# Moving the weight sums of a recursive matrix product from GpSimd to VectorE, and multiplying one pair of column tiles without them

## The chip, the cores and the metric

The kernel runs on one core of one Trainium2 chip. The metric is the device time of one execution in microseconds (us). Three runs of the kernel before took 566.07, 566.41 and 570.07 us; their median is 566.41 us. The profile is one further execution, of 565.62 us.

Five engines work side by side, each through its own queue in a fixed order: TensorE (PE; its weight loads are the row PEld), VectorE (DVE), ScalarE (ACT), GpSimd (POOL) and SyncE (SP, which issues DMA transfers). An instruction that has to wait holds up all behind it on its engine.

## The reference

Three parts follow one another. The first is a landmark attention over 4 batches of 576 tokens and 8 heads. Its 2304 rows of 512 go through a mixture of 8 experts in which a token is computed by one expert alone. The rows that come out go through a gated unit with 1536 hidden columns:

```python
gate = 1.0 / (1.0 + np.exp(-(x @ w_gate)))
val = x @ w_val
return (gate * val @ w_out).astype(np.float32)
```

Here `w_gate` and `w_val` are 512x1536 and `w_out` is 1536x512.

## The kernel before, in words

**Blocks.** A block is the 576 tokens of one batch together with one expert that some of them chose. Only blocks that are needed are computed. In this input there are three: "lead", "1" and "2". For each the kernel runs the expert (`expert_products`) and then the gated unit (`unit_products` or `fast_products`, then `unit_out`). A loop at the end, for further blocks ("b"), is in the program but has no iteration here. I call the gated units of the three blocks unit 0, unit 1 (the middle one) and unit 2.

**Precision.** Each fp32 operand is split into a high part (a cast by ScalarE) and a low part (a subtraction by VectorE). A product is three matmuls: high by high, high by low, low by high (`PASSES`). Weights lie split in six tiles `ws`, in the profile ws_69 to ws_72, ws_2646 and ws_2647. A unit's gate and value weights go through the first four and `w_out` through the last two (`fast_outs`).

**Tiles.** The unit's 1536 columns are 12 column tiles of 128 (`KG` = 12), numbered f, and the tokens two halves of 288. For each f and each half the unit makes a gate product and a value product over the inner dimension of 512, then sigmoid, a multiplication and another split into a `slot` tile (`gated_rows`). `unit_out` multiplies these with `w_out` into five accumulators `acc` in PSUM; the five are stored by indirect DMA from GpSimd (`store_out`, line 1089).

**The recursive product.** Unit 0 works plainly. Units 1, 2 and b (`FAST`) take two column tiles together, the pair p, as a 2x2 block product with 7 multiplications in place of 8 (`chain`, line 915). For each pair and for gate and value apart there are 7 pieces of weight, listed in `CHAIN`: three are blocks of the weights, one is a block that was overwritten by the sum S2 = A21 + A22 - A11 (`fast_combine`, line 767), and three more, s1, s3 and s4, are each the sum or difference of a block and S2. `fast_piece` (line 779) makes them in `temp` tiles, in the profile `rows`, before it splits them. All these sums are done by GpSimd, 128x256 elements each: 24 for the S2 of all pairs, once, and 36 for each fast unit. The moving operand too is summed, four sums "t1" to "t4" made by VectorE (`turn`). Split pieces go through 8 places in the four `ws` tiles, in turn: piece n waits until piece n - 8 has been multiplied (the event `used_...`).

A chain needs three PSUM banks of the three there are (`mm`); for the value chain of the first pair it uses three accumulators instead (`spare`). Results of the seven products are added up by VectorE and ScalarE (`fast_one`, `fast_five`, `fast_two`, `fast_gate`).

**What sets the order.** Every piece of work is a Python generator that names the engine and the events that it needs. `Streams.go` takes, step by step, the one that can start first by a table of costs and due times, and emits its instructions. The order on each engine is thus fixed when the program is built; on the chip each engine runs its list and waits where an operand is late. In the profile nearly all instructions have line 103, the helper that emits them, so the tile names tell them apart.

## Time and profile before

| what | value |
|---|---|
| median of three runs | 566.41 us |
| the profiled execution | 565.62 us |
| its span, first to last instruction | 563.7 us |
| mean granted TensorE clock | 0.981 of full speed |
| unit 1, first product of its block to the expert of block 2 | 272.1 to 407.9 us |
| expert of block 2 | 407.9 to 447.5 us |
| unit 2, up to the last matmul | 447.5 to 555.9 us |

Times in the views are us from the first instruction. A busy time of an engine is the time in which one of its instructions ran; a wait is idle time just before an instruction, put down to whatever released it last. An instruction of VectorE or ScalarE may be shown starting a little before the one ahead of it ends, so that a row of n merged instructions is shorter than n times one of them.

### The profile page before, as it was taken

How to read it: one execution, taken by the hardware profiler on the slowest of the kernel's cores; microseconds unless marked ns; L12 is line 12 of the kernel's file. 1: busy time of each engine (PE TensorE's matmuls, PEld its weight loads, DVE VectorE, ACT ScalarE, POOL GpSimd, SP SyncE). 2: the span in 40 equal slices, each digit the busy share in tenths (PEclk: the TensorE clock that was granted, in tenths of full speed). 3: DMA queues.
4: the chain of work that ended last, by engine and by line, in shares of the span. 5: the costliest groups of instructions: out<-in, count | busy, mean ns of one | idle time of the engine just before them, and what ended most of it. 6: DMA issues, size and time to landing. Idle time of an engine off the chain costs nothing.

```text
span 563.7 us, 12531 instructions
## 1 busy us (share of the span) xinstructions
PE 530.5 (94%) x4734; PEld 470.6 (83%) x4734; DVE 438.3 (78%) x1056; ACT 305.9 (54%) x777; POOL 162.8 (29%) x196
## 2 busy tenths in 40 slices
PE   7999979999999999999794999999999989999994
PEld 3468868889999899999684889998789989999983
DVE  7887767878599999898879898755375798888541
ACT  1645524454677777673454666743263467677331
POOL 2425844334311200000618643100240133331003
PEclk9999989999999999999887999999999999999998
DMA  8548885966345455530420000000530000000002
GB/s 314 193 138 307 295 297 152 316 198 211 121 150 187 153 192 180 187 117 2 169 77 19 1 1 2 1 1 0 185 126 2 1 1 2 1 1 1 1 1 90
DMA packets 33188, 61.90 MB, mean 110 GB/s; under 512 B 3584, under 2 KB 13440, under 8 KB 33120
## 3 DMA queue, kind: packets, MB, share of 16 engines
q1 hardware_dynamic: 32016, 57.48, 30.9%
q0 software_dynamic: 1104, 3.54, 1.8%
q8 instruction: 39, 0.64, 0.5%
q14 instruction: 29, 0.24, 0.1%
HBM read 47.76 MB, written 13.25 MB: 108 GB/s over the span
## 4 chain that ended last, share of the span: by engine, by line
PE 64%; DVE 15%; issue 11%; DMA 4%; ACT 3%; POOL 2%; SPq 1%; POOLq 0%; ACTq 0%; DVEq 0%
PE mm L103 42%; PE acc L103 14%; DVE ws L103 5%; DVE slot L103 2%; PE pz L103 1%; DMA w_raw<-in_moe_w 1%; DVE work L103 1%; PE pv L103 1%; DMA slot<-in_k 1%; ACT ws L103 1%; PE idle L103 1%; DMA x_rows<-xa 1%; DVE cvt_v L103 1%; DVE cvt_g L103 1%; PE pc L103 1%
## 5 line engine op out<-in xcount | busy, mean ns | idle before, releaser
L103 PE MATMUL mm<-xa,ws 128*128 128x288 f32 x966 | 139.9, 297 | 1.1 <-DVE slot L103 0.6
L103 PEld LDWEIGHTS mm<-xa,ws 128*128 128x128 f32 x966 | 132.6, 188 | 6.3 <-DVE slot L103 1.4
L103 PE MATMUL acc<-ws,slot 128*128 128x512 f32 x504 | 128.7, 396 | 2.4 <-DVE ws L103 1.7
L103 PE MATMUL mm<-slot,ws 128*128 128x288 f32 x840 | 124.0, 301 | 5.7 <-DVE ws L103 4.0
L103 PEld LDWEIGHTS mm<-slot,ws 128*128 128x128 f32 x840 | 116.4, 191 | 9.8 <-DVE ws L103 4.7
L103 PEld LDWEIGHTS acc<-ws,slot 128*128 128x128 f32 x504 | 91.2, 189 | 20.0 <-DVE ws L103 2.0
L103 PE MATMUL mm<-xb,ws 128*128 128x288 f32 x558 | 87.5, 301 | 1.9 <-ACT work L103 0.9
L103 PEld LDWEIGHTS mm<-xb,ws 128*128 128x128 f32 x558 | 79.7, 191 | 5.5 <-ACT work L103 1.3
L103 DVE TENSOR_TENSOR slot<-work,slot 128x288 fp32r<-128x288 f32 (+1 forms) x80 | 34.3, 453 | 14.5 <-ACT slot L103 14.1
L103 ACT CAST slot<-work 128x288 fp32r<-128x288 f32 x56 | 22.6, 431 | 38.4 <-PE acc L103 23.3
L103 DVE TENSOR_TENSOR ws<-wg_res,ws 128x256 fp32r<-128x256 f32 (+1 forms) x60 | 31.3, 536 | 10.7 <-ACT ws L103 10.2
L103 DVE TENSOR_TENSOR work<-mm,work 128x288 f32<-128x288 f32 x64 | 28.9, 452 | 11.2 <-PE mm L103 9.1
L103 ACT COPY work<-mm 128x288 f32<-128x288 f32 x66 | 26.1, 396 | 20.0 <-DVE mm L103 11.7
L103 DVE TENSOR_TENSOR ws<-rows,ws 128x256 fp32r<-128x256 f32 x72 | 34.5, 496 | 1.9 <-ACT ws L103 1.9
L103 POOL TENSOR_TENSOR rows<-wg_res,wg_res 128x256 f32<-128x256 f32 x24 | 19.8, 839 | 47.8 <-DVE ws L103 47.8
L103 DVE TENSOR_TENSOR ws<-wv_res,ws 128x256 fp32r<-128x256 f32 (+1 forms) x60 | 32.7, 557 | 1.0 <-ACT ws L103 0.9
L1089 POOL DMA_INDIRECT out<-rows,idx_lead x5 | 5.3, 1063 | 93.5 <-DVE rows L103 86.1
L103 ACT CAST ws<-wg_res 128x256 fp32r<-128x256 f32 (+1 forms) x60 | 25.4, 447 | 11.6 <-PE mm L103 8.6
L103 ACT CAST ws<-wv_res 128x256 fp32r<-128x256 f32 (+1 forms) x60 | 26.0, 447 | 10.0 <-PE mm L103 4.3
L103 POOL TENSOR_TENSOR ws<-w_raw,ws 128x512 fp32r<-128x512 f32 x16 | 20.9, 1307 | 26.9 <-ACT ws L103 21.1
L103 ACT CAST ws<-rows 128x256 fp32r<-128x256 f32 x72 | 27.6, 404 | 1.3 <-POOL rows L103 1.1
L103 ACT ACTIVATE slot<-mm 128x288 fp32r<-128x288 f32 x48 | 19.5, 409 | 16.2 <-PE mm L103 15.6
(248 smaller groups left out, 802.8 us busy)
## 6 DMA issues: line engine op xcount, KB each, us to landing
w_raw<-in_moe_w SPq DMA_DIRECT2D x48, 256.0 KB, 3.5
raw_g<-in_moe_w_gate SPq DMA_DIRECT2D x12, 512.0 KB, 3.6
raw_v<-in_moe_w_val SPq DMA_DIRECT2D x12, 512.0 KB, 3.5
raw_o<-in_moe_w_out SPq DMA_DIRECT2D x12, 512.0 KB, 4.0
out<-zeros SPq DMA_DIRECT2D x18, 256.0 KB, 5.1
vs<-in_v SPq DMA_DIRECT2D x8, 512.0 KB, 5.1
slot<-in_q SPq DMA_DIRECT2D x8, 288.0 KB, 5.5
slot<-in_k SPq DMA_DIRECT2D x8, 288.0 KB, 6.0
```

The lines of the kernel that those rows point to most:

```text
L103: return getattr(self.engine, op)(*args, **kwargs)
L1089: scatter = nc.gpsimd.indirect_dma_start(out[:, :], bass.IndirectOffsetOnAxis(ap=idx[0:n, c : c + 1], axis=0), o[0:n], None, bounds_check= ...
```

## The change

All sums move from GpSimd to VectorE: the 24 for S2 and the 36 of each fast unit. The first pair of column tiles of unit 1 (block "1", f below 2) is no longer a recursive product: a new function `pair` makes it of eight plain products, each over one column tile, one half of the tokens, gate or value. Its weights are the blocks themselves (eight pieces instead of 14), so it needs neither S2 nor the sums of the moving operand. S2 of pair 0, which overwrites the block A21, is made after unit 1 has split that block. Since unit 1 now uses 78 pieces and not 84, the places of the pieces and the tiles that the next expert takes first shift (`spread`, `ROLL_TWO`, `fast_out`), and the spare accumulators are no longer used in unit 1. Units 2 and b keep their seven products in all pairs.

```diff
@@ -678,7 +678,7 @@
     ROLL_LEAD = [i % 4 for i in range(KF // 2 + 2 * KD)]
 
     ROLL = [0, 1, 4, 5, 2, 3] * 2
-    ROLL_TWO = [2, 3, 4, 5, 0, 1] * 2
+    ROLL_TWO = [3, 0, 4, 5, 1, 2] * 2
 
     def unit_tiles(b, f):
 
@@ -722,21 +722,24 @@
     def unit_gate(b, f, half, pts):
 
         sl = slice(half * HT, (half + 1) * HT)
-        yield "act", "sg"
-        sg = tmp.tile([128, HT], F32, tag="sg", name="sg")
+        kind = "work" if b in FAST else "sg"
+        yield "act", kind
+        sg = work() if b in FAST else tmp.tile([128, HT], F32, tag="sg", name="sg")
         on.act.activation(sg, pts[0][:, 0:HT], AF.Sigmoid)
         run.release("bank")
         yield ("dve",)
         on.dve.tensor_tensor(sg, pts[1][:, 0:HT], sg, ALU.mult)
         run.release("bank")
         yield from gated_rows(b, f, half, sg)
-        run.release("sg")
+        if b in FAST:
+            works.append(sg)
+        run.release(kind)
         run.done(f"low_{b}{f}{half}")
 
     def gated_rows(b, f, half, sg):
         sl = slice(half * HT, (half + 1) * HT)
         k = f % 4
-        head = half == (f % 2 if b in FAST else 0)
+        head = half == (0 if plain(b, f) else f % 2)
         yield "act", *([f"slot{k}"] if head else [f"gv_{b}{f}"])
         if head:
             gvs[b, f] = slot(k).rearrange("p a t -> p (a t)")
@@ -757,7 +760,7 @@
 
     def spread(b):
 
-        return 4 if b in ("1", "2") else 0
+        return {"1": 4, "2": 6, "b": 0}[b]
 
     def fast_tile(b, n):
         j = (n + spread(b)) % 8
@@ -766,27 +769,30 @@
 
     def fast_combine():
 
-        for p in range(KG // 2):
+        for p in (*range(1, KG // 2), 0):
             for nm, res in zip("gv", (wgs, wvs)):
                 s2, a22, a11 = res[2 * p + 1][:, 0:2], res[2 * p + 1][:, 2:4], res[2 * p][:, 0:2]
-                begun = [f"used_1{14 * (p - 2)}"] if p > 1 else []
-                yield "pool", f"narrow_o{KG - 1}", f"u_0{nm}{2 * p}", f"u_0{nm}{2 * p + 1}", *begun
-                on.pool.tensor_tensor(s2, s2, a22, ALU.add)
-                yield ("pool",)
-                on.pool.tensor_tensor(s2, s2, a11, ALU.subtract)
+                begun = [f"u_1{nm}02"] if p == 0 else [f"narrow_o{KG - 1}"] if p == 1 else [f"used_1{14 * (p - 2)}"]
+                yield "dve", f"u_0{nm}{2 * p}", f"u_0{nm}{2 * p + 1}", *begun
+                on.dve.tensor_tensor(s2, s2, a22, ALU.add)
+                yield ("dve",)
+                on.dve.tensor_tensor(s2, s2, a11, ALU.subtract)
                 run.done(f"s2_{nm}{p}")
+
+    def plain(b, f):
+        return b not in FAST or (b == "1" and f < 2)
 
     def fast_piece(b, p, nm, i, n):
 
         res = {"g": wgs, "v": wvs}[nm]
         a11, a12, s2, a22 = (res[2 * p + j // 2][:, j % 2 * 2 : j % 2 * 2 + 2] for j in range(4))
         w = fast_tile(b, n)[1]
-        what = CHAIN[i]
+        what = ("11", "12", "s2", "22")[i] if plain(b, 2 * p) else CHAIN[i]
         if what in ("s1", "s3", "s4"):
             x, y, op = {"s1": (s2, a11, ALU.add), "s3": (a22, s2, ALU.subtract), "s4": (a12, s2, ALU.subtract)}[what]
-            yield "pool", "temp"
+            yield "dve", "temp"
             src = temps.pop(0)
-            on.pool.tensor_tensor(src, x, y, op)
+            on.dve.tensor_tensor(src, x, y, op)
         else:
             src = {"11": a11, "12": a12, "s2": s2, "22": a22}[what]
         yield ("act",)
@@ -804,15 +810,17 @@
         run.spawn(fast_outs(b), run.urgency)
         n = 0
         for p in range(KG // 2):
-            for nm in "gv":
-                for i in range(len(CHAIN)):
+            ways = [(nm, i) for nm in "gv" for i in range(len(CHAIN))]
+            if plain(b, 2 * p):
+                ways = [(nm, i) for j in range(2) for nm in "gv" for i in range(2 * j, 2 * j + 2)]
+            for nm, i in ways:
                     k, _ = fast_tile(b, n)
-                    yield None, f"s2_{nm}{p}", *([f"ws{k}"] if n < 8 and n % 2 == 0 else [f"used_{b}{n - 8}"] if n >= 8 else [])
+                    yield None, *([] if plain(b, 2 * p) else [f"s2_{nm}{p}"]), *([f"ws{k}"] if n < 8 and n % 2 == 0 else [f"used_{b}{n - 8}"] if n >= 8 else [])
                     run.spawn(fast_piece(b, p, nm, i, n), run.urgency)
                     n += 1
 
     def fast_out(b, f):
-        return 4 + f % 2 if f < KG - 2 else (4 - spread(b)) // 2 + f % 2
+        return 4 + f % 2 if f < KG - 2 else {"1": 1, "2": 1, "b": 2}[b] + f % 2
 
     def fast_outs(b):
         for f in range(KG):
@@ -912,16 +920,42 @@
 
         left = [KG]
 
+        count = (KG - 2 if plain(b, 0) else KG) * 7 + (8 if plain(b, 0) else 0)
+
+        def pair():
+            n = 0
+            for f in range(2):
+                tiles = {(nm, j): n + 2 * i + j for i, nm in enumerate("gv") for j in range(2)}
+                for half in range(2):
+                    pts = []
+                    for nm in "gv":
+                        for j in range(2):
+                            yield "pe+", *(["bank"] if j == 0 else []), f"u_{b}{nm}0{2 * f + j}", f"expert_{expert}", *[f"y_{expert}{2 * j + k}{half}" for k in range(2)]
+                            if j == 0:
+                                pts.append(bank())
+                            _, w = fast_tile(b, tiles[nm, j])
+                            for kk in range(2):
+                                for a, c in PASSES:
+                                    on.pe.matmul(
+                                        pts[-1][:, 0:HT], w[:, a, kk], x[:, c, 2 * j + kk, half * HT : (half + 1) * HT],
+                                        start=(j == 0 and kk == 0 and (a, c) == PASSES[0]), stop=(j == 1 and kk == 1 and (a, c) == PASSES[-1]),
+                                    )
+                            if half == 1:
+                                run.done(f"used_{b}{tiles[nm, j]}")
+                    run.spawn(unit_gate(b, f, half, list(pts)), run.urgency)
+                n += 4
+            run.done(f"banks_{b}v0")
+
         def chain(p, nm, order):
             q = f"{b}{nm}{p}"
             spare = p == 0 and nm == "v"
-            before = [f"expert_{expert}", *([f"f_{b}{d}1" for d in (1, 3)] if spare else [])] if p == 0 else [f"banks_{b}{'v' if nm == 'g' and p > 1 else 'g'}{p - (nm == 'g')}"]
+            before = [f"expert_{expert}", *([f"f_{b}{d}1" for d in (1, 3)] if spare else [])] if p == 0 else [f"banks_{b}{'v' if nm == 'g' and (p > 1 or plain(b, 0)) else 'g'}{p - (nm == 'g')}"]
             pts = {}
             for i, (pt, what, needs) in enumerate((
                 ("x", "11", before), ("z", "t1", []), ("x", "21", [f"one_{q}"]), ("z", "22", [f"five_{q}"]),
                 ("y", "t2", []), ("y", "t3", [f"two_{q}"]), ("y", "t4", [f"c22_{q}"]),
             )):
-                new, n = pt not in pts, order * len(CHAIN) + i
+                new, n = pt not in pts, order * 7 + i - (6 if plain(b, 0) else 0)
                 yield "pe+", *(([f"acc{len(pts)}"] if spare else ["bank"]) if new else []), f"u_{q}{i}", *ready(what), *needs
                 if new:
                     pts[pt] = (accs[len(pts)] if spare else bank())[:, 0:HT]
@@ -933,7 +967,7 @@
                             start=(new and kk == 0 and (a, c) == PASSES[0]), stop=(kk == 1 and (a, c) == PASSES[-1]), skip_group_check=True,
                         )
                 run.done(f"used_{b}{n}")
-                if n >= 7 * KG - 8 and n % 2:
+                if n >= count - 8 and n % 2:
                     run.release(f"ws{k}")
                 x, y, z = (f"acc{j}" if spare else "bank" for j in (0, 2, 1))
                 if i == 0:
@@ -955,7 +989,10 @@
                 run.done(f"unit_{b}")
 
         yield (None,)
-        for p in range(KG // 2):
+        if plain(b, 0):
+            left[0] -= 2
+            run.spawn(pair(), run.urgency)
+        for p in range(1 if plain(b, 0) else 0, KG // 2):
             for i, nm in enumerate("gv"):
                 run.spawn(chain(p, nm, 2 * p + i), run.urgency)
```

**TensorE at the start of unit 1.** `mm<-xb` are products of the block's own tokens, `mm<-slot_40..` those of the sums t1 to t4, `acc<-ws_26..` the output products of unit 0. Before:

```order
L103 MATMUL mm<-xa,ws_72 128x288 x12
L103 MATMUL mm<-xb,ws_71 128x288 x6
L103 MATMUL acc_2691<-ws_2646,slot_3982 128x512 x2
L103 MATMUL acc_2689<-ws_2646,slot_3982 128x512 x3
L103 MATMUL mm<-slot_4018,ws_71 128x288 x6
L103 MATMUL mm<-xb,ws_72 128x288 x6
L103 MATMUL acc_2691<-ws_2647,slot_4070 128x512 x2
L103 MATMUL acc_2689<-ws_2647,slot_4070 128x512 x3
L103 MATMUL acc_2687<-xb,ws_70 128x288 x6
L103 MATMUL mm<-xb,ws_72 128x288 x6
L103 MATMUL mm<-slot_4019,ws_69 128x288 x6
```

Now:

```order
L103 MATMUL mm<-xa,ws_72 128x288 x12
L103 MATMUL mm<-xb,ws_71 128x288 x12
L103 MATMUL mm<-xb,ws_72 128x288 x12
L103 MATMUL mm<-xb,ws_71 128x288 x12
L103 MATMUL mm<-xb,ws_72 128x288 x12
L103 MATMUL mm<-xb,ws_69 128x288 x12
L103 MATMUL mm<-xb,ws_70 128x288 x12
L103 MATMUL mm<-xb,ws_69 128x288 x12
L103 MATMUL mm<-xb,ws_70 128x288 x12
L103 MATMUL acc_2691<-ws_2646,slot_3982 128x512 x2
L103 MATMUL mm<-xb,ws_71 128x288 x6
L103 MATMUL mm<-slot_4018,ws_71 128x288 x6
```

The eight rows of 12 matmuls are the plain pair. They stand ahead of the first product of a sum, which before came as the second product of the unit.

**VectorE at the same place.** `rows<-` are the sums s1, s3 and s4, `wg_res<-` and `wv_res<-` those of S2, `ws<-` the low parts of the split pieces. Before:

```order
L103 TENSOR_TENSOR ws_69<-wv_res_2652,ws_69 128x256
L103 TENSOR_TENSOR ws_70<-wg_res_2654,ws_70 128x256
L103 TENSOR_TENSOR ws_71<-wg_res_2654,ws_71 128x256
L103 TENSOR_TENSOR ws_72<-wg_res_2657,ws_72 128x256
L103 TENSOR_TENSOR ws_69<-wg_res_2657,ws_69 128x256
L103 TENSOR_TENSOR ws_70<-rows_4015,ws_70 128x256
L103 TENSOR_TENSOR ws_2647<-wo_res_2653,ws_2647 128x512
L103 TENSOR_TENSOR work_4253<-acc_2689,work_4253 128x288
```

Now:

```order
L103 TENSOR_TENSOR wg_res_2663<-wg_res_2663 128x256
L103 TENSOR_TENSOR ws_71<-wg_res_2654,ws_71 128x256
L103 TENSOR_TENSOR rows_4015<-wg_res_2657,wg_res_2654 128x256
L103 TENSOR_TENSOR slot_4276<-work_4012,slot_4276 128x288
L103 TENSOR_TENSOR wg_res_2663<-wg_res_2663,wg_res_2660 128x256
L103 TENSOR_TENSOR ws_71<-rows_4015,ws_71 128x256
L103 TENSOR_TENSOR ws_72<-wg_res_2654,ws_72 128x256
L103 TENSOR_TENSOR rows_4015<-wg_res_2654,wg_res_2657 128x256
L103 TENSOR_TENSOR work_4014<-mm,work_4014 128x288
L103 TENSOR_TENSOR wv_res_2664<-wv_res_2664 128x256
L103 TENSOR_TENSOR ws_72<-rows_4015,ws_72 128x256
L103 TENSOR_TENSOR slot_4276<-work_4014,slot_4276 128x224
```

The sums now stand in VectorE's queue between the splits, the multiplications of gate and value and the splits of these.

**GpSimd at the same place.** Before, from the end of unit 0 on:

```order
L1089 DMA out<-rows_4015,idx_lead 2304x512
L1089 DMA out<-rows_4016,idx_lead 2304x512
L103 TENSOR_TENSOR rows_4015<-wg_res_2651,wg_res_2648 128x256
L103 TENSOR_TENSOR rows_4015<-wg_res_2648,wg_res_2651 128x256
L103 TENSOR_TENSOR rows_4016<-wg_res_2651 128x256
L103 TENSOR_TENSOR rows_4016<-wv_res_2652,wv_res_2649 128x256
L103 TENSOR_TENSOR wg_res_2663<-wg_res_2663 128x256
L103 TENSOR_TENSOR wg_res_2663<-wg_res_2663,wg_res_2660 128x256
```

Now:

```order
L1126 DMA out<-rows_4015,idx_lead 2304x512
L1126 DMA out<-rows_4016,idx_lead 2304x512
L1126 DMA out<-rows_4017,idx_lead 2304x512
L1126 DMA out<-rows_4015,idx_lead 2304x512
L1126 DMA out<-rows_4016,idx_lead 2304x512
L1126 DMA out<-rows_4017,idx_one 2304x512
L1126 DMA out<-rows_4015,idx_one 2304x512
```

Line 1126 is line 1089 of before. Between the stores of unit 0 and those of unit 1 GpSimd has nothing left to do.

## Rows read from the trace of the kernel before

**Rows 1.** The page's first part: busy time, share of the span and instructions of each engine.

```profile
PE 530.5 (94%) x4734; PEld 470.6 (83%) x4734; DVE 438.3 (78%) x1056; ACT 305.9 (54%) x777; POOL 162.8 (29%) x196
```

**Rows 2.** Busy time by stage: from:to, us, each engine's busy us (count), PEclk, DMA.

```profile
272.10:338.00 65.90, 52.74 (x321) 47.82 (x320) 60.14 (x110) 37.62 (x105) 39.58 (x48) 0.90 0.17 57
338.00:372.70 34.70, 34.70 (x245) 33.59 (x245) 27.13 (x70) 23.49 (x66) 7.46 (x9) 1.00 0.01 2
...
407.90:447.50 39.60, 38.90 (x289) 38.19 (x288) 26.62 (x53) 18.39 (x43) 8.84 (x10) 1.00 0.16 53
447.50:460.30 12.80, 10.99 (x77) 10.21 (x76) 11.62 (x26) 8.90 (x27) 2.98 (x4) 1.00 0.00 0
460.30:523.40 63.10, 63.10 (x439) 60.75 (x439) 53.14 (x138) 45.34 (x128) 20.31 (x24) 1.00 0.01 1
```

**Rows 3.** Timeline of TensorE: start, us, instructions merged, [idle before <-releaser].

```profile
243.15 20.05 PE L103 MATMUL mm<-xa,ws 128*128 128x288 f32 x150
...
280.94 1.33 PE L103 MATMUL mm<-slot,ws 128*128 128x288 f32 x4 [4.04 <-DVE ws L103]
...
297.75 0.73 PE L103 MATMUL acc<-ws,slot 128*128 128x512 f32 x2 [1.69 <-DVE ws L103]
...
303.16 1.33 PE L103 MATMUL acc<-slot,ws 128*128 128x288 f32 x4 [4.41 <-DVE ws L103]
...
382.97 12.89 PE L103 MATMUL acc<-ws,slot 128*128 128x512 f32 x56
395.80 1.95 PE L103 MATMUL mm<-w_raw,fold_now 64*32 64x128 f32 x64
```

**Rows 4.** Busy time in stretches of 5 us, as in Rows 2, around both stops.

```profile
275.00:280.00 5.00, 1.90 (x11) 1.45 (x9) 5.00 (x4) 1.32 (x4) 4.92 (x8) 0.90 0.93 313
280.00:285.00 5.00, 4.05 (x14) 3.77 (x15) 3.87 (x11) 3.71 (x11) 1.40 (x2) 0.50 0.69 245
...
300.00:305.00 5.00, 1.84 (x7) 1.84 (x8) 5.00 (x6) 0.80 (x2) 4.92 (x7) 0.50 0.00 0
305.00:310.00 5.00, 4.03 (x24) 3.45 (x24) 5.00 (x10) 2.12 (x7) 3.60 (x5) 0.87 0.00 0
```

**Rows 5.** Timeline of VectorE, columns as in Rows 3.

```profile
266.52 0.82 DVE L103 TENSOR_TENSOR work<-xb 128x288 f32<-128x288 f32 x2
...
273.98 4.25 DVE L103 TENSOR_TENSOR work<-work,work 128x288 f32<-128x288 f32 x1
...
282.45 0.41 DVE L103 TENSOR_TENSOR ws<-wg_res,ws 128x256 fp32r<-128x256 f32 x1
...
283.13 0.74 DVE L103 TENSOR_TENSOR ws<-rows,ws 128x256 fp32r<-128x256 f32 x2
...
297.85 4.38 DVE L103 TENSOR_TENSOR slot<-work,slot 128x224 fp32r<-128x224 f32 x2 [0.15 <-ACT slot L103]
...
544.53 1.90 DVE L103 TENSOR_TENSOR ws<-wo_res,ws 128x512 fp32r<-128x512 f32 x3
```

**Rows 6.** Timeline of GpSimd, columns as in Rows 3.

```profile
274.42 1.45 POOL L103 TENSOR_TENSOR rows<-wg_res,wg_res 128x256 f32<-128x256 f32 x2
```

**Rows 7.** VectorE's forms from 275 to 345 us: xcount, busy us, mean ns, idle before.

```profile
L103 DVE TENSOR_TENSOR ws<-rows,ws 128x256 fp32r<-128x256 f32 x24 | 12.5, 527 | 0.3 <-ACT ws L103 0.3
L103 DVE TENSOR_TENSOR ws<-wv_res,ws 128x256 fp32r<-128x256 f32 x15 | 9.7, 662 | 0.0
L103 DVE TENSOR_TENSOR ws<-wg_res,ws 128x256 fp32r<-128x256 f32 x15 | 9.0, 621 | 1.2 <-ACT ws L103 1.0
...
L103 DVE TENSOR_TENSOR slot<-work,slot 128x224 fp32r<-128x224 f32 x6 | 6.2, 1041 | 0.8 <-ACT slot L103 0.8
```

**Rows 8.** The same from 460 to 560 us.

```profile
L103 DVE TENSOR_TENSOR ws<-rows,ws 128x256 fp32r<-128x256 f32 x30 | 13.1, 461 | 0.8 <-ACT ws L103 0.8
...
L103 DVE TENSOR_TENSOR slot<-work,slot 128x224 fp32r<-128x224 f32 x12 | 4.6, 385 | 4.0 <-ACT slot L103 3.8
```

**Rows 9.** Timeline of VectorE, the last product of the block before unit 2.

```profile
447.71 0.71 DVE L103 TENSOR_TENSOR work<-mm,gate_now 128x288 f32<-128x288 f32 x1 [0.63 <-PE mm L103]
```

## The prediction, made before the changed kernel was run

> **What bounds the kernel now.** I read first the busy time of the engines. TensorE is busy for 530.5 of 563.7 us [rows 1], so a change can win little more than TensorE's idle time and what its clock loses, unless it takes matmuls away, and this one adds some.
>
> Then I read the stages, to see where TensorE idles. From 272.1 to 338.0 us, the first half of unit 1, it is busy for 52.74 of 65.90 us, so 13.2 us are idle, and the granted clock is 0.90 there. In the second half of unit 1 and in the middle of unit 2 it does not idle at all, although GpSimd makes the same sums there; the expert of block 2 loses 0.7 us and the start of unit 2 1.8 us [rows 2].
>
> Then the timeline of TensorE, to see what ended the idle time. Three stops, of 4.04, 1.69 and 4.41 us, make 10.1 of the 13.2 us, and each ended with a VectorE split of weights [rows 3]. Behind both long ones stands a stretch of 5 us at a granted clock of 0.50, that is at 1.2 in place of 2.4 GHz: half of the 4.05 and of the 1.84 us busy there was lost, 2.9 us, and the stretches at 0.90 and 0.87 give 0.2 and 0.5 us more [rows 4]. With 3.6 us of clock the first half of unit 1 loses 16.8 us in all.
>
> Last I read VectorE and GpSimd at the stops. One VectorE subtraction that reads two SBUF tiles started at 273.98 us and took 4.25 us, and two at 297.85 took 4.38; undisturbed, two of 288 columns take 0.82 us, so one about 0.45 [rows 5]. The long one started just before a run of GpSimd sums [rows 6]: in the five us from 275 to 280 GpSimd ran 8 instructions without a break and VectorE got through 4 [rows 4]. From 275 to 345 us the three forms of `ws` splits take 527, 662 and 621 ns on average and the 224-wide split 1041 ns [rows 7]; alone they take 410 ns [rows 5] and 385 ns [rows 8]. With the one of 4.25 us the excess is 24 x 0.117 + 15 x 0.252 + 15 x 0.211 + 6 x 0.656 + 3.8 = 17.5 us. So GpSimd's sums hold VectorE up, VectorE's splits come late, and TensorE stops.
>
> **The change, part by part.** *The sums on VectorE.* A 128x256 subtraction takes 0.41 us, and two in a row 0.74 [rows 5], so one more costs 0.34 us of the queue; in the same way 288 columns cost 0.82 - 0.45 = 0.37 us and 512 columns 0.61, from three in 1.90 [rows 5]; for a split of 224 and 64 together I take 0.43, in proportion. In unit 1 VectorE gets 23 sums for S2 and 30 for s1, s3, s4: 53 x 0.34 = 18.0 us. The excess of 17.5 us goes, since GpSimd runs only stores there, so in unit 1 the move is even for VectorE. What it wins is that no sum waits behind seven others, at 39.58/48 = 0.82 us each [rows 2], for splits that TensorE waits for.
>
> The Trainium skill ("SBUF — State Buffer", section "SBUF: two separate sides") says that VectorE with two SBUF inputs and GpSimd share one pair of ports, and that the loser is blocked for the whole of the other's instruction. By that the subtraction of 4.25 us would have been held for one sum, 0.74 us, and taken 1.2; the trace shows it held through several, and I go by the trace. By the rule alone the two long stops would be 3 us shorter each, as much less would be won, and the sum would be 561.6 us.
>
> *The plain pair.* Eight products of 12 matmuls in place of 14 of six: 96 - 84 = 12 matmuls more, each 20.05/150 = 0.133 us [rows 3]: 1.6 us on TensorE's path. On VectorE it saves six splits (14 pieces to 8) and six additions in PSUM, 6 x 0.34 + 6 x 0.37 = 4.3 us. It puts 12.8 us of products that need only single blocks ahead of the first sum.
>
> *Does VectorE keep up in unit 1?* I count the changed order from the last sum of `xb` halves. It stood at 266.52 + 0.37 = 266.9 us [rows 5]; now one S2 sum more and one 512-wide split less are ahead of it, so about 266.6. Up to the last piece stand 131 instructions of 256, 72 of 288, 10 of 512 and 8 pairs of 224 and 64: 80.7 us. Behind it TensorE has 6 matmuls of 0.133 us, 89 of 12.89/56 = 0.23 and twice the 64 small ones of the next expert, 1.95 us each [rows 3]: 25.2 us. So VectorE alone would end unit 1 at 266.6 + 80.7 + 25.2 = 372.5 us if it never waited, at 392.7 if it waited a fifth of the time. TensorE without any loss ends at 407.9 - 16.8 + 1.6 = 392.7 us. TensorE stays the bound as long as VectorE is packed to 80%; in the stalled stretch it was busy for 60.14 of 65.90 us, 91% [rows 2].
>
> The narrowest place is the first `w_out` split of unit 1. VectorE reaches its end after 45.7 us, at 312.3 without a wait and at 317.4 at 90%; TensorE starts on the pair at 272.1 + 18 x 0.133 = 274.5, behind the last products of unit 0, and wants the split after 43.0 us of products, at 317.5. At 85% TensorE would stop for 2.9 us there. The pair frees its eight places only at 274.5 + 6.4 = 280.9 and at 287.3 us, which holds VectorE up by some 2 us more. I take 2.0 us for that, 0.5 for the pair's own start (its value pieces come just as the gate product ends) and 1.5 for waits inside chains, half of what is left of the 13.2 us beside the three stops: **4.0 us stay** in unit 1. The bounds are 0, if everything fits, and 6.7, if VectorE is packed to 75%: 266.6 + 107.6 + 25.2 = 399.4.
>
> *Unit 2.* It gets 36 sums, 12.2 us, and gets little back: its splits take 461 ns [rows 8], some 50 over 410, in 69 instructions of three forms 3.5 us. At its start VectorE counts from the last gated product, at 447.71 us [rows 9], 9.1 us to the piece that TensorE wants 8.0 us after its own start at 447.5; that product ends 0.9 us after this start, so TensorE waits 2.0 us by this, 3.0 at 90%, where it waits 1.8 now. After that VectorE has 68.4 us in the queue up to the last piece and TensorE 84.8, so 81%; now it is busy for 53.14 of 63.10 us, 84%, and TensorE never idles [rows 2]. I take **1.5 us more** in unit 2; bounds 0, and 4.4 at 75%: 448.4 + 91.2 + 20.7 us of output products = 560.3 in place of 555.9.
>
> *The rest.* The 0.7 us in block 2's expert follow a VectorE write while GpSimd makes six sums; I take half, 0.4 us, as won. The eight S2 sums in unit 0 were hidden by TensorE's work there, which never stopped for long: 0. The stores come at the same points of the accumulators, and the tail is the same: 0.
>
> **The sum:** 565.6 - 16.8 + 1.6 + 4.0 + 1.5 - 0.4 = **555.5 us**. This is made against the profiled execution, 565.62 us, which lies 0.8 us under the median of 566.41; I leave that out.
>
> **The rivals.** *Everything is won.* Nothing stays in units 1 and 2: 565.6 - 16.8 + 1.6 - 0.7 = 549.7 us. For it speaks that TensorE idles nowhere in the second half of unit 1 [rows 2]; against it the narrow place above. Chance 0.15.
>
> *A mere swap.* VectorE pays for the sums what it is freed of, and TensorE goes on following it. Then unit 1 gets shorter only by what VectorE saves: 17.5 - 18.0 + 4.3 = 3.8 us, and unit 2 pays 1.5: 563.3 us, no change that can be told. Against it stands that TensorE's stops were bursts, two runs of sums, and not a steady lack of VectorE. The Trainium skill ("Perfetto Trace Analysis", section "Optimizing Scalar/DVE Operations") says of GpSimd and VectorE that moving work between them might not help, since they share a port; this would be the swap. By my count of VectorE's total the trace agrees; by the stops it does not. Chance 0.15.
>
> *VectorE becomes the bound.* Its queue is in order, and a sum now waits there behind a split that waits for ScalarE, which waits for TensorE. If that packs it to 70%, unit 1 ends at 266.6 + 115.3 + 25.2 = 407.1, and unit 2 at 448.4 + 97.7 + 20.7 = 566.8, 10.9 later: 565.6 - 0.8 + 10.9 = 575.7 us, slower. It decides from 73%, where the loss of unit 2 (6.9) passes the gain of unit 1 (5.4). Against it stand the 91 and 84% of now. Chance 0.08; packed to 74 to 76%, 559 to 564 us, 0.10.
>
> That the change does not do what it says is out: the order shows every sum on VectorE and the pair ahead.
>
> **How the numbers follow.** The forecast, 551 to 559 us, has 0.52, and the rivals the rest. The range reaches from 548.7, under the case in which everything is won, to 562.5, which takes in most of the poorly packed cases and some of the swap. One per cent, 5.7 us, is about what can be told from no change here: faster by over 1% means under 560.7 us. Forecast, full gain and half of the poor packing make 0.72; the swap and the other half 0.20; the slower rival 0.08.
>
> **What would show it.** In the changed profile no VectorE subtraction longer than 1 us in unit 1, `ws` splits at about 410 ns, no TensorE stop over 2 us between 272 and 340 us, and no stretch at 0.50 clock; TensorE's first product of unit 2 about 11 us earlier. VectorE should be busy near 85% in units 1 and 2. I am wrong if TensorE waits 2 us or more at the first `w_out` product of unit 1, or if its waits for `ws` splits in unit 2 add up to over 4 us.

## The result, and the profile after

The changed kernel took 547.47 us (median of 4 runs, 545.15 to 547.57) against 566.24 us for the kernel before on the same chip; the ratio is 0.965, with a 95% interval of 0.960 to 0.970. It is 18.8 us faster. The forecast was 555.5 us with a range from 548.7, so the direction was right and the gain came out 8 us larger, a little past the range. The profiled execution took 547.57 us, 18.0 less than the one of before.

The first part of the page of the changed kernel, to be laid beside [rows 1]:

```profile
PE 525.2 (96%) x4746; PEld 468.7 (86%) x4746; DVE 430.4 (79%) x1134; ACT 303.9 (56%) x765; POOL 83.4 (15%) x100
```

GpSimd lost 96 instructions, all of its sums. VectorE gained 78 net and is busy for 7.9 us *less* than before.

By the landmarks that the prediction used (the first product of a block's stage, in the timeline of TensorE), the 18.0 us lie here:

| stretch | before | after | change |
|---|---|---|---|
| up to the last products of unit 0 | 272.12 | 271.64 | -0.5 |
| unit 1 | 135.69 | 118.29 | -17.4 |
| expert of block 2 | 39.71 | 39.83 | +0.1 |
| unit 2, to the end of the last matmul | 108.35 | 107.67 | -0.7 |
| the rest | 9.75 | 10.14 | +0.4 |

The stages of the changed kernel in windows (columns as in [rows 2], where each has its counterpart):

```profile
271.64:337.60 65.96, 65.83 (x462) 63.45 (x461) 60.91 (x173) 45.05 (x123) 5.43 (x5) 1.00 0.17 58
389.93:429.76 39.83, 38.98 (x289) 38.28 (x288) 26.70 (x55) 18.39 (x43) 1.97 (x3) 1.00 0.16 53
442.50:505.00 62.50, 62.50 (x437) 60.36 (x436) 57.52 (x164) 45.91 (x127) 0.00 (x0) 1.00 0.00 1
```

In the first half of unit 1 TensorE is idle for 0.13 us where it was for 13.2, and the granted clock is 1.00 where it was 0.90. VectorE is busy for 60.91 of 65.96 us there: as full as before (60.14 of 65.90), but now TensorE hardly waits for it.

TensorE's timeline at the start of unit 1 and at the place that the prediction called narrowest, the first `w_out` products (the answer to [rows 3]):

```profile
271.64 2.56 PE L103 MATMUL mm<-xa,ws 128*128 128x288 f32 x18
274.04 12.88 PE L103 MATMUL mm<-xb,ws 128*128 128x288 f32 x96
286.76 0.62 PE L103 MATMUL acc<-ws,slot 128*128 128x512 f32 x2
...
316.89 1.96 PE L103 MATMUL acc<-ws,slot 128*128 128x512 f32 x6
...
437.42 1.06 PE L103 MATMUL mm<-xb,ws 128*128 128x288 f32 x6 [0.85 <-DVE work L103]
```

VectorE's split of that first `w_out` tile, and the busy times from the prediction's starting point up to there:

```profile
316.68 0.68 DVE L103 TENSOR_TENSOR ws<-wo_res,ws 128x512 fp32r<-128x512 f32 x1
```

```profile
266.60:316.89 50.29, 50.29 (x352) 48.56 (x351) 45.34 (x127) 33.62 (x95) 4.48 (x4) 1.00 0.21 70
```

The plain pair runs as one block of 96 matmuls without a stop. The first `w_out` product of unit 1's own (316.89) has no wait before it; the 0.13 us of idle time lie inside that row, whose second product starts at 317.41, behind the split's end at 317.36. The longest wait left from unit 1 on is one of 0.85 us at the start of unit 2.

In the 5-us windows around those times (the answer to [rows 4]) the clock never falls, and VectorE is busy all the time in one of the three and nearly all in another:

```profile
280.00:285.00 5.00, 5.00 (x40) 5.00 (x39) 3.81 (x13) 2.45 (x8) 0.00 (x0) 1.00 0.64 236
305.00:310.00 5.00, 5.00 (x40) 5.00 (x39) 5.00 (x15) 3.57 (x12) 0.00 (x0) 1.00 0.00 0
315.00:320.00 5.00, 4.87 (x31) 4.23 (x30) 4.91 (x14) 3.73 (x11) 1.13 (x1) 1.00 0.15 56
```

VectorE's groups by form from 275 to 345 us (the answer to [rows 7]):

```profile
L103 DVE TENSOR_TENSOR ws<-rows,ws 128x256 fp32r<-128x256 f32 x26 | 10.6, 416 | 0.4 <-ACT ws L103 0.4
L103 DVE TENSOR_TENSOR ws<-wg_res,ws 128x256 fp32r<-128x256 f32 x21 | 8.7, 416 | 2.0 <-ACT ws L103 2.0
L103 DVE TENSOR_TENSOR ws<-wv_res,ws 128x256 fp32r<-128x256 f32 x20 | 8.0, 417 | 0.8 <-ACT ws L103 0.8
L103 DVE TENSOR_TENSOR slot<-work,slot 128x224 fp32r<-128x224 f32 x6 | 2.3, 382 | 0.0
```

The same splits that took 527, 621, 662 and 1041 ns take 416, 416, 417 and 382: each form is back at the time it takes alone, and no VectorE instruction of unit 1 takes as much as 1 us.

### The profile page after: what moved, and what is told of

It reads as the page before. It is cut to its first block, busy times and chain, and to the rows that moved or that the text cites. A ratio compares the mean times of both kernels' runs of the same rounds, so it can differ in the third digit from the quotient of the medians.

```text
span 545.7 us, 12491 instructions
## 1 busy us (share of the span) xinstructions
PE 525.2 (96%) x4746; PEld 468.7 (86%) x4746; DVE 430.4 (79%) x1134; ACT 303.9 (56%) x765; POOL 83.4 (15%) x100
## 5 line engine op out<-in xcount | busy, mean ns | idle before, releaser
L103 PE MATMUL mm<-slot,ws 128*128 128x288 f32 x816 | 118.6, 299 | 0.0
L103 PEld LDWEIGHTS mm<-slot,ws 128*128 128x128 f32 x816 | 112.0, 189 | 2.7 <-issue 0.5
L103 PE MATMUL mm<-xb,ws 128*128 128x288 f32 x636 | 96.9, 297 | 1.1 <-DVE work L103 0.9
L103 PEld LDWEIGHTS mm<-xb,ws 128*128 128x128 f32 x636 | 88.9, 188 | 4.3 <-DVE work L103 1.1
L103 DVE TENSOR_TENSOR slot<-work,slot 128x288 fp32r<-128x288 f32 (+2 forms) x80 | 26.7, 362 | 12.7 <-ACT slot L103 12.4
L103 DVE TENSOR_TENSOR ws<-wg_res,ws 128x256 fp32r<-128x256 f32 (+1 forms) x60 | 28.1, 470 | 5.6 <-ACT ws L103 5.3
L103 DVE TENSOR_TENSOR ws<-wv_res,ws 128x256 fp32r<-128x256 f32 (+1 forms) x60 | 27.6, 471 | 2.6 <-ACT ws L103 2.6
L103 DVE SCALAR_TENSOR_TENSOR slot<-mm,slot 128x288 fp32r<-128x288 f32 x48 | 21.2, 451 | 8.5 <-ACT slot L103 8.1
L103 DVE TENSOR_TENSOR ws<-rows,ws 128x256 fp32r<-128x256 f32 x66 | 26.7, 416 | 0.9 <-ACT ws L103 0.9
L1126 POOL DMA_INDIRECT out<-rows,idx_two x5 | 4.8, 967 | 142.5 <-ACT rows L103 140.8
```

The source lines that it names most:

```text
L103: return getattr(self.engine, op)(*args, **kwargs)
L1126: scatter = nc.gpsimd.indirect_dma_start(out[:, :], bass.IndirectOffsetOnAxis(ap=idx[0:n, c : c + 1], axis=0), o[0:n], None, bounds_check= ...
```

## The experiments

Two theories stood at the start. **A:** GpSimd's sums hold VectorE up, and that alone cost the time. **B:** the chains lacked lead; the plain pair gives it, and where the sums run matters little.

All runs in one table. The ratio is to the kernel before on the same chip; units 1 and 2 are lengths in the profiled execution between the landmarks above; VectorE is its busy time in the whole span.

| kernel | median us | ratio, 95% interval | unit 1 | unit 2 | VectorE |
|---|---|---|---|---|---|
| before | 566.24 | 1 | 135.69 | 108.35 | 438.3 |
| after | 547.47 | 0.965 [0.960, 0.970] | 118.29 | 107.67 | 430.4 |
| after, again | 547.68 | 0.964 [0.959, 0.970] | 118.28 | 107.63 | 429.5 |
| sums only | 545.42 | 0.961 [0.952, 0.970] | 117.71 | 107.61 | 435.4 |
| sums only, again | 546.09 | 0.961 [0.956, 0.966] | 117.69 | 107.66 | 435.2 |
| pair only | 561.28 | 0.987 [0.983, 0.992] | 130.53 | 108.35 | 430.7 |
| only S2 moved | 558.02 | 0.985 [0.977, 0.993] | 126.24 | 108.36 | 434.4 |
| only s1, s3, s4 moved | 556.34 | 0.979 [0.972, 0.986] | 126.52 | 107.63 | 439.1 |
| unit 2's sums on GpSimd | 549.94 | 0.966 [0.959, 0.973] | 118.30 | 108.32 | 427.6 |
| sums twice on VectorE | 555.64 | 0.978 [0.971, 0.984] | 122.19 | 111.82 | 451.2 |
| idle fills on GpSimd | 549.33 | 0.967 [0.958, 0.976] | 118.83 | 107.66 | 429.6 |
| idle copies on GpSimd | 560.00 | 0.987 [0.980, 0.994] | 124.04 | 114.58 | 447.6 |
| idle sums, half | 567.15 | 1.000 [0.995, 1.004] | 127.36 | 118.84 | 454.4 |
| idle sums | 596.19 | 1.050 [1.040, 1.060] | 143.46 | 130.95 | 484.1 |

Lengths between landmarks repeat to some 0.05 us where the stage is the same and TensorE hardly stops in it (unit 1 in after, after again and the run with unit 2 on GpSimd: 118.29, 118.28, 118.30; unit 2 in four programs with its sums on GpSimd: 108.32 to 108.36), while unit 1 *starts* anywhere from 268.9 to 274.8 us. So one profile tells a tenth of a us there, where the whole time does not tell 2 us. That this holds where TensorE stops is not shown: each such program has one profile, that of the pair alone is the fastest of its ten runs (558.00 us) and that of only S2 moved is 4 us under its median. Their lengths of unit 1 may be on the short side.

**1. The sums alone.** The kernel before with two engine names changed, in `fast_piece` and in `fast_combine`:

```diff
-            yield "pool", "temp"
+            yield "dve", "temp"
...
-            on.pool.tensor_tensor(src, x, y, op)
+            on.dve.tensor_tensor(src, x, y, op)
...
-                on.pool.tensor_tensor(s2, s2, a22, ALU.add)
+                on.dve.tensor_tensor(s2, s2, a22, ALU.add)
```

> The kernel before with all sums of weights (s1, s3, s4 and S2) on VectorE, and nothing else: no plain pair, S2 sums in the old order. Theory A (GpSimd's sums hold VectorE up, and that alone cost the 19 us): the stops at 281 and 303 and the half clock go, 12 matmuls (1.6 us) less than in the changed kernel, but the first chain now waits on its S2 sums: 546 to 550 us. Theory B (the plain pair gives the lead that the chains lacked; where the sums run matters little): the first chain still stops for about 4 us and the clock falls once: 553 to 566 us.

Measured 545.42 us, 0.6 under theory A's range and far from B's. Page and one window of 30 us of this kernel, then all that TensorE's timeline shows as a wait in unit 1 beyond 0.2 us:

```profile
PE 524.2 (96%) x4734; PEld 467.6 (86%) x4734; DVE 435.4 (80%) x1152; ACT 309.2 (57%) x777; POOL 83.4 (15%) x100
```

```profile
295.00:325.00 30.00, 30.00 (x207) 28.76 (x207) 30.00 (x89) 22.88 (x64) 0.00 (x0) 1.00 0.01 2
```

```profile
275.65 1.40 PE L103 MATMUL acc<-ws,slot 128*128 128x512 f32 x5 [0.55 <-ACT work L103]
```

The move of the sums is the whole gain. VectorE does 96 instructions more than before and is busy for 2.9 us less; it ran without a gap from 295 to 325 us and TensorE did not notice.

**2. The pair alone.** The changed kernel with the same lines turned back to GpSimd:

```diff
-            yield "dve", "temp"
+            yield "pool", "temp"
```

> The changed kernel with all sums of weights back on GpSimd: the plain pair, the new order of the S2 sums and the rest of the change stay. Theory A: 48 GpSimd sums in unit 1 hold VectorE as before, TensorE stops again and the clock falls: 557 to 566 us. Theory B: 547 to 550 us.

Measured 561.28 us, as A said. VectorE's forms of this kernel from 275 to 345 us, and its stretch with the longest stop:

```profile
L103 DVE TENSOR_TENSOR ws<-rows,ws 128x256 fp32r<-128x256 f32 x23 | 14.4, 635 | 1.3 <-ACT ws L103 1.3
L103 DVE TENSOR_TENSOR work<-mm,work 128x288 f32<-128x288 f32 x23 | 10.3, 449 | 2.9 <-PE mm L103 2.7 <-ACT work L103 0.2
L103 DVE TENSOR_TENSOR work<-work,work 128x288 f32<-128x288 f32 x6 | 3.9, 649 | 0.1
L103 DVE TENSOR_TENSOR mm<-mm,work 128x288 f32<-128x288 f32 x7 | 3.2, 460 | 0.2
```

```profile
310.00:315.00 5.00, 4.44 (x32) 4.22 (x32) 5.00 (x8) 4.03 (x11) 5.00 (x7) 1.00 0.06 22
315.00:320.00 5.00, 2.66 (x17) 2.18 (x17) 5.00 (x9) 0.71 (x2) 4.64 (x6) 0.99 0.01 2
320.00:325.00 5.00, 4.57 (x26) 4.23 (x25) 5.00 (x9) 2.15 (x6) 4.64 (x6) 0.67 0.00 0
```

VectorE gets through 8 or 9 instructions in 5 us, where the changed kernel's windows from 305 to 345 us have 14 to 16: TensorE stops, and the clock falls behind the stop, as it did in [rows 4]. With the sums on GpSimd the pair does win some 5.2 us of unit 1 (135.69 to 130.53, one profile each), but only of a loss that the other half of the change removes.

**3. GpSimd instructions for which nobody waits.** Into the changed kernel, behind each split of a piece in the fast units:

```diff
+        if b in FAST:
+            for kk in range(2):
+                nc.gpsimd.tensor_tensor(ident, a22[:, kk], w[:, 1, kk].bitcast(F32), ALU.add)
```

`ident` is read by no one any more; the order of the other engines stays as in the changed kernel.

> The changed kernel, and beside each split of a weight tile in units 1 and 2 two GpSimd sums of 128x128 whose result nobody reads (about 0.5 us each, so some 75 us of GpSimd in unit 1 and 80 in unit 2, against 39.6 in 66 us before). Theory A: VectorE's instructions are held for microseconds without anybody waiting for a sum; VectorE had 5 us to spare in 272 to 338, so TensorE stops: 557 to 585 us. Theory B, and any in which the chain from sum to split is what cost the time: 546.5 to 549 us.

Measured 596.19 us: theory A's direction, and 11 us past its range. I had not expected a loss in unit 2 as large as in unit 1. GpSimd was nearly full in this run, so a backlog could have had a part: a piece's place is rewritten only when GpSimd has read it. A waits view of unit 1 puts 2.5 us of VectorE's time to that and none of ScalarE's, and the next but one run settles it.

In place of the sums, fills with zeros behind a copy of one column:

```diff
-                nc.gpsimd.tensor_tensor(ident, a22[:, kk], w[:, 1, kk].bitcast(F32), ALU.add)
+                nc.gpsimd.memset(ident, 0.0)
```

> As the run before, but GpSimd fills the same tile with zeros (two fills of 128x128 for each weight tile behind a copy of one column) and so reads no operands. If any GpSimd instruction in on-chip memory holds VectorE: 555 to 585 us. If what holds VectorE is GpSimd's reading of two operands: 546.5 to 549 us.

Measured 549.33 us, just past the second range. GpSimd's groups and VectorE's `ws<-rows` split of this run, 275 to 345 us:

```profile
L808 POOL MEMSET ident<- 128x128 f32 x134 | 27.5, 205 | 7.8
L806 POOL COPY ident<-ws 128x1 f32<-128x1 f32 x67 | 22.9, 341 | 7.5 <-DVE ws L103 3.7
```

```profile
L103 DVE TENSOR_TENSOR ws<-rows,ws 128x256 fp32r<-128x256 f32 x26 | 10.6, 415 | 0.4 <-POOL ident L808 0.4
```

GpSimd is busy for 50 of 70 us, more than with the sums of before, and the split takes 415 ns: undisturbed. Neither the fills nor the copies of one column hold it.

One sum of 128x128 for each piece in place of two:

> As the run with the idle GpSimd sums with one sum of 128x128 for each split instead of two, so that GpSimd is about 45% busy and never behind. Theory A (sums hold VectorE in proportion to their time): half of VectorE's extra 54 us, of which units 1 and 2 can hide about 10: 555 to 575 us. If the 596 us came from GpSimd's backlog, for which the next split of the same tile must wait: 547 to 550 us.

567.15 us, inside theory A's range: the loss does not need a backlog. VectorE's split here, 275 to 345 us, takes 486 ns for the 415 beside fills:

```profile
L103 DVE TENSOR_TENSOR ws<-rows,ws 128x256 fp32r<-128x256 f32 x24 | 11.4, 486 | 0.4 <-ACT ws L103 0.2
```

And copies, which read one operand:

```diff
-                nc.gpsimd.tensor_tensor(ident, a22[:, kk], w[:, 1, kk].bitcast(F32), ALU.add)
+                nc.gpsimd.tensor_copy(ident, w[:, 1, kk].bitcast(F32))
```

> As the run with the idle GpSimd sums, but each of the two instructions beside a split is a copy of 128x128 (one operand is read, not two), its result unused. If any GpSimd instruction that reads on-chip memory holds VectorE: 557 to 590 us, near the 596 us of the sums. If it takes two operands: 546.5 to 550 us, as with the fills.

560.00 us: in the first range, but at its bottom, not near the 596 of the sums. One operand is enough to hold VectorE, for less. From 275 to 345 us, GpSimd's copies, then two VectorE forms of the same run:

```profile
L807 POOL COPY ident<-ws 128x128 f32<-128x128 f32 x128 | 45.7, 357 | 17.3 <-DVE ws L103 10.4
```

```profile
L103 DVE TENSOR_TENSOR ws<-rows,ws 128x256 fp32r<-128x256 f32 x24 | 11.4, 485 | 0.4 <-POOL ident L807 0.2
L103 DVE TENSOR_TENSOR work<-mm,work 128x288 f32<-128x288 f32 x24 | 10.7, 446 | 0.1
```

The split with both operands in SBUF is slower by 69 ns on average, the addition that reads PSUM takes 446 as ever.

**4. Which sums.** The kernel before with only the S2 sums moved, and with only the others moved, each by the lines of the first experiment that belong to it.

> The kernel before with only the 24 sums S2 on VectorE; s1, s3, s4 stay on GpSimd. If the loss goes by GpSimd's busy time alone (17 of the 36 sums that it made in 275 to 345 were S2): half of the 19 us comes back, 554 to 559 us. If what costs is a burst of sums back to back, which the S2 sums are: 547 to 552 us.

> The kernel before with only s1, s3, s4 on VectorE; the 24 sums S2 stay on GpSimd. By busy time alone: 554 to 559 us. If the burst of S2 sums is what costs: 559 to 565 us.

Measured 558.02 and 556.34 us, both inside the ranges for "by busy time". In the one profile of each, unit 1 gets shorter by 9.5 and by 9.2 us, and by 18.0 when both move: the two halves roughly add up, and neither kind of sum is the culprit alone. In the second of these runs the S2 sums, left alone on GpSimd, make one large stop with a fall of the clock behind it (its windows from 290 us); in the first the loss comes in nine waits of 0.2 to 1.2 us.

```profile
290.00:295.00 5.00, 2.05 (x9) 1.18 (x9) 5.00 (x10) 1.52 (x4) 4.83 (x6) 1.00 0.00 0
295.00:300.00 5.00, 3.68 (x15) 2.99 (x14) 5.00 (x9) 1.28 (x3) 4.19 (x5) 0.51 0.00 0
```

**5. Unit 2, and how far VectorE can be filled.** First the changed kernel with `"dve" if b == "1" else "pool"` as the engine of s1, s3 and s4:

> The changed kernel with the 36 sums s1, s3, s4 of unit 2 alone back on GpSimd; unit 1 keeps all on VectorE. By the prediction's step (VectorE is the more loaded place in unit 2, 1.5 us): 546 us. By theory A with the waits that unit 2 shows in the run with all sums on GpSimd (1.78 us against 1.42 in the changed kernel): 547.5 to 549 us. If unit 2 loses as unit 1 did: 553 to 560 us.

Measured 549.94 us, a little past the middle range. Unit 2 itself gets 0.65 us longer (108.32 for 107.67). Most of the rest of that profiled execution's difference is one wait of TensorE, 2.75 us in block 2's expert. Behind it stands a long hold like those of [rows 5]: a VectorE split that reads two SBUF tiles, otherwise 0.69 us, takes 3.96 us. It lasts through five of six sums that GpSimd, behind a store, already makes for unit 2. TensorE's row, VectorE's, then GpSimd's:

```profile
398.90 9.78 PE L103 MATMUL mm<-xa,ws 128*128 128x288 f32 x66 [2.75 <-DVE slot L103]
```

```profile
394.52 3.96 DVE L103 TENSOR_TENSOR ws<-w_raw,ws 128x512 fp32r<-128x512 f32 x1
```

```profile
393.77 1.42 POOL L103 TENSOR_TENSOR rows<-wg_res,wg_res 128x256 f32<-128x256 f32 x2
395.15 0.75 POOL L103 TENSOR_TENSOR rows<-wg_res 128x256 f32<-128x256 f32 x1
395.84 1.40 POOL L103 TENSOR_TENSOR rows<-wv_res,wv_res 128x256 f32<-128x256 f32 x2
397.21 0.71 POOL L103 TENSOR_TENSOR rows<-wv_res 128x256 f32<-128x256 f32 x1
```

Then each sum made twice:

```diff
             on.dve.tensor_tensor(src, x, y, op)
+            yield ("dve",)
+            on.dve.tensor_tensor(src, x, y, op)
```

> The changed kernel with each sum s1, s3, s4 made twice on VectorE (66 more instructions of 0.417 us, 12.5 us in unit 1 and 15 in unit 2). If VectorE can be filled to the last tenth before TensorE waits (5 us spare in 272 to 338, 5 us in 442 to 505): 558 to 564 us. If it can be filled to 80% only, as the prediction had it: all 27.5 us come through, 570 to 576 us. If the splits are far ahead of their use: 547.5 to 553 us.

Measured 555.64 us, between two ranges: 2.4 us better than the case in which VectorE can be filled to the last tenth, 2.6 worse than that of splits far ahead of their use. Two windows of that run:

```profile
305.00:310.00 5.00, 5.00 (x37) 4.86 (x37) 5.00 (x15) 3.36 (x10) 0.00 (x0) 1.00 0.00 0
310.00:315.00 5.00, 2.76 (x14) 1.85 (x13) 4.94 (x15) 4.23 (x12) 1.43 (x1) 0.97 0.00 0
```

The 66 sums made VectorE's busy time 20.8 us longer, 0.315 us each, and the run 8.2 us longer. TensorE stops here: between the changed kernel and this one lies the load at which VectorE becomes the bound.

**6. Which of the two is better.** Once more, side by side:

> The changed kernel itself, once more, beside the next run on the same chip: 547.5 us.

> The kernel before with all sums of weights on VectorE and no plain pair, once more: 545.5 us. If the plain pair only costs its 12 matmuls, it stays 1.6 to 2.1 us under the changed kernel; if the difference between the first runs was one of chips, the two agree within 0.5 us.

547.68 and 546.09 us. The two intervals overlap, so the whole times do not settle it. The profiles do for the stage: unit 1 is 0.6 us shorter without the pair in both pairs of profiles, though it stops once, for 0.55 us. The version with the sums alone is the simpler one and not slower; a gain of more than 0.6 us over the changed kernel is not shown.

## Why the prediction was right in kind and wrong in size

**Right.** GpSimd's sums holding VectorE was the cause (experiments 1 to 3); no run separates what sums that came late in their chain may have added. The swap on VectorE was even, as counted. The 96 sums held it for 438.3 - (435.4 - 96 x 0.315) = 33.1 us before, 0.345 us for each; doing one costs it 0.315. The working had 0.33 and 0.34. Of the signs named for the changed profile four came: no long subtraction, splits at 416 ns, no stop over 2 us, no half clock. Two did not: VectorE is 92% busy in the first half of unit 1 and in the middle of unit 2 (57.52 of 62.50 us), not 85%, and unit 2 begins 17.8 us earlier, not 11.

The forecast was a gain of 10.1 us against the profiled execution, and 18.0 came. The terms of the 7.9 us between are, as measured: 3.9 and 1.7 and 0.5 in unit 1, 2.2 in unit 2, and 0.5, -0.5 and -0.4 in unit 0, the expert and the tail.

**The step that failed: "4.0 us stay" in unit 1.** Measured, TensorE is idle there for 0.13 us. At the narrowest place the count itself came true: VectorE was busy for 45.34 of 50.29 us, 90%, and its split ended at 317.36 us, where the working has 317.4 for 90%. Wrong was to price the place at 85%, for which the working names no row, and to add waits at the pair's places and inside the chains; no such wait of TensorE came. Beyond that the runs show VectorE filled to 100% for 30 us without a wait of TensorE (experiment 1), and 20.8 us of further work costing only 8.2. The 91% of before, beside which the working sets its shares, was a share of an engine that stood held inside its instructions, and so no measure of how tightly its own work can be packed. This is the 3.9 us.

**"16.8 us" was too small.** Unit 1 without its loss is 117.7 - 0.55 = 117.15 us by experiment 1, so the loss before was 18.5 us. Idle time and clock gave 16.8. Of the 1.7 us between, 0.5 is clock in two windows of the kernel before that the working left out (5.00 x 0.08 and 2.06 x 0.05):

```profile
285.00:290.00 5.00, 5.00 (x31) 4.48 (x30) 3.29 (x5) 1.89 (x6) 2.69 (x3) 0.92 0.22 70
295.00:300.00 5.00, 2.06 (x11) 1.39 (x10) 4.79 (x8) 4.02 (x13) 3.40 (x5) 0.95 0.14 52
```

The other 1.2 us stand in time that the view counts as busy (122.53 us in unit 1, against 117.05 in experiment 1 for the same products); that they are short waits is not shown. Where a like stage without the trouble exists, a length between landmarks is the better measure.

**The pair, "1.6 us".** It costs 118.29 - 117.15 = 1.1 us, and 0.6 net of the 0.55 us stop that it takes away. The working did not ask what it wins by itself: some 5.2 us where GpSimd makes the sums, nothing where VectorE does.

**Unit 2, "+1.5 us".** Measured -0.7, and the run with unit 2 back on GpSimd gives +0.65, so this is real. The same mistake: VectorE, busier there by 4.8 us (84.3 for 79.5 between the landmarks), was taken to make TensorE wait in proportion. It hid all of it.

**Small terms.** Block 2's expert: -0.4 forecast, +0.1 measured, and 39.2 to 40.0 in the other runs, but for the 42.85 of the one with the long hold there, so nothing. Unit 0: 0 forecast, -0.5 measured, inside the scatter of that start.

**The rivals.** "Everything is won" (549.7 us) was nearest, and was given 0.15. "A mere swap" had its premise right and its conclusion wrong. The Trainium skill ("Perfetto Trace Analysis", section "Optimizing Scalar/DVE Operations") says that moving work between these two engines might not help, since they share a port. VectorE's busy time bears the premise out; the time fell by 3.5%. Why equal busy time is not equal time can be read in part from the last experiments together. Put on top of the changed kernel, own work of 20.8 us cost 8.2 (0.39 us for each us), holds by idle copies of 17.2 us cost 12.5 (0.73), holds by idle half sums of 24.0 us cost 19.7 (0.82). These are no fixed prices. By an estimate from busy times, with 0.315 us for each sum, unit 1 of the kernel before had 22.7 us of holds (103.88 us busy, against 98.23 less 54 sums in experiment 1) and lost 18.5; unit 2 with its sums on GpSimd had 5.9 us (79.53 against 84.28 less 34 sums) and lost 0.65. VectorE was 91% busy in the first half of the one and 84% in the middle of the other: the same kind of sum costs next to nothing where VectorE has room. One reason may be that the written order has room planned for VectorE's own work and none for a hold; the order was not rebuilt with holds in its costs, so that stays argued.

**The rule weighed in the prediction.** The Trainium skill ("SBUF — State Buffer", section "SBUF: two separate sides") says that VectorE with two SBUF inputs contends with a GpSimd instruction that reads SBUF, and only with one that does. The runs agree: 415 ns beside fills, 485 beside copies, 486 beside half the idle sums, 635 beside the sums of experiment 2, and 445 to 462 for forms that read PSUM, beside all of them. That the loser waits for the whole of *one* instruction is not what the long holds show (below).

## What to carry to other kernels

Busy time of an engine that shares something can be someone else's instruction. Compare the mean duration of one form in a disturbed and in an undisturbed stretch before reading the share as work, and price the move by holds removed against instructions added. And an engine off the critical path whose order leaves it room can be filled to 100% for tens of us; take a packing limit only from a stretch in which its own work, and not a hold, fills it.

## What the runs showed of the hardware

**Price of a hold.** Taken from the busy times of the pages, for each us that GpSimd was busier VectorE was busier by nothing beside fills (-0.8 for 121.0 us), by 0.15 us beside copies (17.2 for 115.7), by 0.25 and 0.29 beside idle sums (24.0 for 95.0 and 53.7 for 182.9), and by 0.42 beside the sums of before (33.1 for 162.8 - 83.4 = 79.4).

**Long holds.** Where VectorE and GpSimd take turns, a held split takes 0.96 us beside sums of 0.92 (the run with the pair alone, 312 to 316 us). The long ones of the kernel before [rows 5] are another kind. Here is the second by itself, from 297.85 to 301.57 us, and below it GpSimd at that time:

```profile
297.85 3.72 DVE L103 TENSOR_TENSOR slot<-work,slot 128x224 fp32r<-128x224 f32 x1 [0.15 <-ACT slot L103]
```

```profile
296.58 1.24 POOL L1089 DMA_INDIRECT out<-rows,idx_lead  x1 [6.73 <-DVE slot L103]
297.84 1.44 POOL L103 TENSOR_TENSOR rows<-wg_res,wg_res 128x256 f32<-128x256 f32 x2
299.21 0.74 POOL L103 TENSOR_TENSOR rows<-wg_res 128x256 f32<-128x256 f32 x1
299.90 0.73 POOL L103 TENSOR_TENSOR rows<-wv_res,wv_res 128x256 f32<-128x256 f32 x1
300.58 0.72 POOL L103 TENSOR_TENSOR wg_res<-wg_res 128x256 f32<-128x256 f32 x1
301.38 0.76 POOL L103 TENSOR_TENSOR wg_res<-wg_res,wg_res 128x256 f32<-128x256 f32 x1
```

It lasts through five sums, each started before the one ahead is shown to end, and is over at the first gap (301.30 to 301.38), ahead of a sum that needs the result of the last. The hold of 4.25 us ends in the same way. The run with only S2 moved has one more, through the three sums that follow a store; VectorE's row first, then GpSimd's:

```profile
271.78 2.69 DVE L103 TENSOR_TENSOR ws<-wg_res,ws 128x256 fp32r<-128x256 f32 x1
```

```profile
271.06 0.98 POOL L1089 DMA_INDIRECT out<-rows,idx_lead  x1 [0.30 <-ACT ws L103]
272.06 1.46 POOL L103 TENSOR_TENSOR rows<-wg_res,wg_res 128x256 f32<-128x256 f32 x2
273.45 0.73 POOL L103 TENSOR_TENSOR rows<-wg_res 128x256 f32<-128x256 f32 x1
```

The hold of 3.96 us in experiment 5 is a fourth, over at the end of its row of sums. Three of the four began within 0.5 us of an indirect store's end on GpSimd, the fourth 0.76 us behind it. A store and back-to-back sums together are not enough: in the run with the pair alone such rows of sums, from 271.25 and 297.19 us, hold no split for over 1.02 us. What decides stays open; the idle sums, of half the size, gave no hold of over 1 us.
